# Repeating score fills ahead of the real ones, in place of zero-weight passes, in a gated mix of two attentions

## The chip, the cores and the metric

The kernel runs on one core of one Trainium2 chip. Its time is the device time of one execution in microseconds (us). The engines are named as in the profile: PE is TensorE (PEld its weight loads), ACT is ScalarE, DVE is VectorE, POOL is GpSimd and SP is SyncE. A profile adds one execution that was recorded instruction by instruction, and with it the share of its full clock that PE was granted from moment to moment.

## The reference

Two attentions over the same 2048 tokens of width 512, each with 32 heads of 16, are mixed by a gate for each token. Branch A is full attention without a mask, branch B looks at 8 earlier positions at a stride of 2.

```python
x = A_x                                                   # 1 x 2048 x 512, bf16
g = _sigmoid((x * gate_w).sum(-1, keepdims=True))
a = _A_ref(x, A_wqkv, A_wo)       # softmax(q k^T / 4) v over all 2048 keys, 32 heads of 16, then @ wo
b = _B_ref(x, B_wqkv, B_wo)       # the same with keys i, i-2, ... i-14 only, mask where < 0
return g * a + (1 - g) * b
```

Branch A is what costs most. Its scores are cut into units of 128 keys by 512 queries of one head: 16 blocks of keys, 4 chunks of queries and 32 heads make 2048 units. A unit is one matmul with a contraction of 32 rows ("score fill"), then 128 x 512 exponentials, then one matmul with the values (17 columns of weights, 16 of values and one of ones for the softmax's denominator).

## The kernel before

Branch A is worked in 32 periods: a chunk of 512 queries with a group of 4 heads, which is 64 units. The four heads of a group lie in the four row strips of 32 of PE's array (`tile_position=(32 * j, 0)`), so fills of different heads can stream side by side. Most units go to ACT in sets of three (ring A, three PSUM banks) and two (ring B, two banks) in turn: PE fills a ring, ACT takes the exponential of the whole ring in one instruction, and the ring is then free for the next fill. A part of the units ("riders") is filled beside a set into a bank of its own, and DVE takes the exponential there by a polynomial of four instructions. Projections, transposes and branch B's dot products lie in between.

The order of the instructions on each engine is not written by hand. When the program is built, a planner (`Plan`) plays the jobs through with an assumed duration for each step, and every engine's instructions are issued in the order in which the plan starts them. On the chip the engines run through these fixed orders and wait for each other by semaphores; the planned times themselves are not kept. A change of a planned duration can therefore move instructions of any job.

```python
class Plan:
    LAT = {"pe": 0.15, "act": 0.08, "dve": 0.08, "pool": 0.08, "sp": 0.08}
    streamed = deque()
    # ... (cut)
    def quiet(self, window):
        while self.streamed and self.streamed[0][0] < self.now - window:
            self.streamed.popleft()
        return sum(d - 0.11 for _, d in self.streamed)
    # ... (cut: run() picks the next step)
                if isinstance(more, float):
                    x[4] += more                      # a step may say that it takes longer
                if nm == "pe":
                    self.streamed.append((st, x[4]))  # what PE streamed, by the plan
```

The fills of the sets, the exponential, and where the ring comes free:

```python
    MM = 0.22; SW = 0.11; WARM = 0.47      # planned: one stream of 512 columns; a change of tiling

    def qk_mm(out_, p, t, j):
        c_, i = periods[p]
        mm(out_, kt_all[32 * j:32 * j + 32, i, t * 128:(t + 1) * 128], qt_tiles[p][32 * j:32 * j + 32, :],
           True, True, tile_position=(32 * j, 0))
    # ... (cut)
    def act_tail(k, parts, rname, rslot, ring, n):
        # ... (cut)
            A.activation(out=st["pT"][:, 0:n, :], in_=ring[:, 0:n, :], func=ACT.Exp,
                         scale=LN2 / 128.0, bias=-VOFF * LN2 / 128.0)
        yield ("act", k, 0.074 + 0.4267 * n, f)
        yield ("rel", rname, rslot)
    # ... (cut: then pv_job for the units of the set)
    def act_stream():
        while front[0] < NP:
            k = nset[0]
            nset[0] += 1
            rname = "rA" if k % 2 == 0 else "rB"
            slot = yield ("acq", rname, 0)
            want = 3 if k % 2 == 0 else 2
            # ... (cut: picks the units)
            dur = SW + MM

            def f():
                for s_, (p_, t, j) in enumerate(units):
                    qk_mm(ring[:, s_, :], p_, t, j)
                # ... (cut: riders)
            yield ("pe", 0, dur, f)
            yield ("spawn", act_tail(k, parts, rname, slot, ring, len(units)))
```

The matmuls with the values add up in one PSUM bank for each period (`acc`). The bank is opened by four passes with weights of zero (128 in the 32 periods). A fifth such pass may be added in a step, and adds zero to what is there:

```python
    def pv_job(p, items, res, prio, act=True):
        # ... (cut)
            extra = MM * (max(cnt) - 1)
            if P.quiet(3.0) + MM * max(cnt) < WARM * 3.0 and max(row_left[p]) > 0:
                j = max(range(4), key=lambda j_: row_left[p][j_])
                mm(acc[32 * j:32 * j + 32, :], z32[:], ones_t[:], False, False, tile_position=(0, 32 * j))
                extra += MM
                njunk[0] += 1
            return extra
```

## Time and profile before

| | |
|---|---|
| time, median of 3 runs | 944.16 us (941.46 to 947.36) |
| span of the profiled execution | 951.0 us, mean granted PE clock 0.842 |
| busy: ACT / PE / DVE / POOL | 851.9 / 800.1 / 762.0 / 582.7 us |
| sets on ACT | 369 of 3 and 2 units each in turn, 737 in all, 1842 units |
| units on DVE | 206 |
| zero-weight passes | 135, of which 128 open a period |

In the profile the groups of instructions are named by what they write and read: `ring<-qt,kt_all` is a score fill of a set, `w<-qt,kt_all` that of a rider, `pT<-ring` the exponential on ACT, `acc<-pT,vp_all` and `acc<-pd,vp_all` the matmuls with the values, `acc<-ones_t,z` a zero-weight pass. All carry the line of one helper, L252, so they are told apart by these names. A matmul's recorded duration [...]is longer than the time for which it keeps the array; matmuls overlap in the records. The row PEclk has the clock that PE was granted, in tenths of full speed.

### The profile page before, as it was taken

What the parts mean: (1) busy time and instruction counts of PE and PEld (TensorE: products, weight loads), DVE (VectorE), ACT (ScalarE), POOL (GpSimd) and SP (SyncE); (2) the same over time, 40 slices, a digit from 0 to 9 for tenths busy, and PEclk for the clock granted to TensorE, in tenths of its full rate; (3) what the DMA queues carried; (4) which work ended last, traced back from release to release, by engine and by line L of the source; (5) the groups of instructions that cost most, each with busy time, mean ns of one, the idle gap of its engine ahead of it and who ended that gap; (6) DMA issues with size and microseconds to landing.
All of it is one profiled execution on the core that took longest, in us unless ns stands there. A gap on an engine that the chain in (4) does not pass through costs nothing.

```text
span 951.0 us, 14436 instructions
## 1 busy us (share of the span) xinstructions
PE 800.1 (84%) x5415; PEld 233.3 (25%) x5415; DVE 762.0 (80%) x1326; ACT 851.9 (90%) x755; POOL 582.7 (61%) x543
## 2 busy tenths in 40 slices
PE   2889989988888888888978888888888988788986
PEld 0333433322222221222222222222122222222221
DVE  3568888868896899788886988788988789898784
ACT  0489899989999999899999989889989989999994
POOL 4005886347984999498949693919567662947000
PEclk9999999979879977778689967768788977876795
DMA  9004010121013303003030310203010230300000
GB/s 261 6 2 155 1 45 1 56 100 57 1 57 102 108 3 100 1 1 100 1 100 12 111 45 12 90 1 101 1 56 5 69 95 1 100 1 1 1 2 22
DMA packets 50007, 47.10 MB, mean 50 GB/s; under 512 B 9984, under 2 KB 47360, under 8 KB 49936
## 3 DMA queue, kind: packets, MB, share of 16 engines
q1 hardware_dynamic: 46240, 41.98, 14.6%
q10 hardware_dynamic: 3696, 4.20, 1.5%
q8 instruction: 42, 0.69, 0.3%
q14 instruction: 29, 0.24, 0.1%
HBM read 37.75 MB, written 6.32 MB: 46 GB/s over the span
## 4 chain that ended last, share of the span: by engine, by line
ACT 49%; PE 27%; issue 18%; DVE 4%; DMA 2%; SPq 0%; ACTq 0%; DVEq 0%
ACT pT L252 48%; PE w L252 11%; PE ring L252 9%; PE acc L252 7%; DMA xT<-in_A_x_dram 2%; DVE ta L252 2%; DVE pd L252 1%; ACT lg L252 0%; DVE kt_all L252 0%; DVE qt L252 0%; DVE vp_all L252 0%; DVE osb L252 0%; DMA out_dram<-osb 0%; SPq L252 0%; DVE accS L252 0%
## 5 line engine op out<-in xcount | busy, mean ns | idle before, releaser
L252 ACT ACTIVATE pT<-ring 128x1536 bf16<-128x1536 f32 x737 | 847.9, 1289 | 74.9 <-PE w L252 34.3
L252 PE MATMUL ring<-qt,kt_all 32*128 32x512 bf16 x1842 | 333.1, 444 | 115.2 <-ACT pT L252 107.4
L252 DVE SCALAR_TENSOR_TENSOR ta<-ta,w 128x512 f32<-128x512 f32 x412 | 278.2, 682 | 6.8
L252 PE MATMUL acc<-pT,vp_all 128*17 128x512 bf16 x1842 | 272.9, 450 | 0.4 <-ACT pT L252 0.2
L252 POOL TENSOR_TENSOR prod<-prod 128x512 f32<-128x512 f32 (+1 forms) x208 | 240.2, 1168 | 6.3
L252 POOL TENSOR_TENSOR prod<-vsh,lg 128x512 f32<-128x512 bf16 x128 | 136.6, 1099 | 174.0 <-issue 102.3
L252 POOL TENSOR_TENSOR prod<-ksh,qb 128x512 f32<-128x512 bf16 x128 | 143.6, 1154 | 104.0 <-DMA ksh<-kv_scr 94.1
L252 PEld LDWEIGHTS <-kt_all 32*128 32x128 bf16 x2048 | 92.3, 94 | 428.4 <-issue 421.8
L252 DVE TENSOR_SCALAR ta<-w 128x512 f32<-128x512 uint16 x206 | 141.4, 687 | 42.2 <-PE w L252 40.0
L252 DVE SCALAR_TENSOR_TENSOR pd<-ta,w 128x512 uint16<-128x512 f32 x206 | 139.8, 680 | 3.1
L252 PE MATMUL w<-qt,kt_all 32*128 32x512 bf16 x206 | 94.0, 458 | 0.0
L252 PE MATMUL acc<-pd,vp_all 128*17 128x512 bf16 x206 | 86.7, 475 | 0.0
L252 PEld LDWEIGHTS <-vp_all 128*17 128x17 bf16 x2048 | 46.2, 90 | 113.3 <-issue 111.8
L252 PE MATMUL w<-xT,wkp 128*128 128x512 bf16 x128 | 37.7, 423 | 19.0 <-DMA xT<-in_A_x_dram 17.2
L252 PE MATMUL w<-bw,xT 128*128 128x512 bf16 x192 | 51.4, 392 | 0.5 <-DVE otok L252 0.2
L252 PE MATMUL w<-xT,wqp 128*128 128x512 bf16 x128 | 50.2, 536 | 0.0
L252 DVE TENSOR_SCALAR absq<-w 128x512 int16<-128x512 int16 x32 | 22.1, 691 | 26.3 <-PE w L252 26.3
L252 DVE TENSOR_SCALAR kt_all<-w,kbias 128x512 bf16<-128x512 f32 x32 | 23.9, 748 | 23.5 <-PE w L252 23.4
L252 PEld LDWEIGHTS <-xT 128*128 128x128 bf16 x512 | 32.7, 103 | 37.0 <-issue 23.8
L252 DVE TENSOR_SCALAR qt<-w,qbias 128x512 bf16<-128x512 f32 x32 | 23.9, 748 | 14.9 <-PE w L252 14.9
L252 DVE COPY accS<-acc 128x512 f32<-128x512 f32 x32 | 22.0, 687 | 10.2 <-PE acc L252 10.2
L252 PE MATMUL w<-identf,accS 128*128 128x128 f32 x128 | 24.7, 324 | 3.7 <-DVE qt L252 2.7
(70 smaller groups left out, 412.5 us busy)
## 6 DMA issues: line engine op xcount, KB each, us to landing
ksh<-kv_scr SPq DMA_DIRECT2D x16, 1024.0 KB, 5.7
vsh<-kv_scr SPq DMA_DIRECT2D x16, 1024.0 KB, 6.8
kv_scr<-kvs SPq DMA_DIRECT2D x16, 256.0 KB, 2.0
out_dram<-osb SPq DMA_DIRECT2D x16, 128.0 KB, 1.8
bw<-in_B_wqkv_dram ACTq DMA_DIRECT2D x1, 1536.0 KB, 13.9
wraw<-in_A_wqkv_dram ACTq DMA_DIRECT2D x2, 512.0 KB, 5.5
wv<-in_A_wqkv_dram ACTq DMA_DIRECT2D x1, 512.0 KB, 9.2
bwo<-in_B_wo_dram ACTq DMA_DIRECT2D x1, 512.0 KB, 7.8
```

The source lines that it names most:

```text
L252: return chain_on(self._key, f(*a, **k))
```

## The change

The zero-weight pass inside a period goes. In its place the fill of a set may be issued twice: first over `n` columns, then over all 512. Both write the same banks with the same weights and the same queries, and the second overwrites the first, so that the computation is unchanged. The number of columns is the plan's shortage: how much less than 1.64 us PE would have streamed within the last 2.5 us, with `cur` for what it is about to stream before it next runs idle (one stream for a fill of three, three for a fill of two), in whole blocks of 64 columns and at most 512. The aim is to keep PE streaming in the stretches where it has little to do, as that of the zero-weight passes was.

```diff
+    REACH = 2.5
+    BUSY = 1.64
-    def quiet(self, window):
-
-        while self.streamed and self.streamed[0][0] < self.now - window:
+    def lack(self, cur):
+
+
+        while self.streamed and self.streamed[0][0] + self.streamed[0][1] < self.now - self.REACH:
             self.streamed.popleft()
-        return sum(d - 0.11 for _, d in self.streamed)
+        have = sum(min(d - 0.11, s + d - self.now + self.REACH) for s, d in self.streamed)
+        return self.BUSY - have - cur
 ...
+    def warm_cols(cur):
+
+        n = min(QW, -(-int(P.lack(cur) * 2400.0) // 64) * 64)
+        if n < 64:
+            return 0
+        njunk[0] += n / QW
+        return n
 ...
-    def qk_mm(out_, p, t, j):
+    def qk_mm(out_, p, t, j, n=QW):
         c_, i = periods[p]
-        mm(out_, kt_all[32 * j:32 * j + 32, i, t * 128:(t + 1) * 128], qt_tiles[p][32 * j:32 * j + 32, :],
+        mm(out_, kt_all[32 * j:32 * j + 32, i, t * 128:(t + 1) * 128], qt_tiles[p][32 * j:32 * j + 32, 0:n],
            True, True, tile_position=(32 * j, 0))
 ...
             extra = MM * (max(cnt) - 1)
-            if P.quiet(3.0) + MM * max(cnt) < WARM * 3.0 and max(row_left[p]) > 0:
-                j = max(range(4), key=lambda j_: row_left[p][j_])
-                mm(acc[32 * j:32 * j + 32, :], z32[:], ones_t[:], False, False, tile_position=(0, 32 * j))
-                extra += MM
-                njunk[0] += 1
             return extra
 ...
             def f():
+                n = warm_cols(MM if len(units) == 3 else 3 * MM)
+                if n:
+                    for s_, (p_, t, j) in enumerate(units):
+                        qk_mm(ring[:, s_, 0:n], p_, t, j, n)
                 for s_, (p_, t, j) in enumerate(units):
                     qk_mm(ring[:, s_, :], p_, t, j)
 ...
+                return n / 2400.0
             yield ("pe", 0, dur, f)
```

## The prediction

> **What bounds the kernel now.** I first read the page: busy shares, the row of PE's clock, and the chain that ended last.

> ```profile
> PE 800.1 (84%) x5415; PEld 233.3 (25%) x5415; DVE 762.0 (80%) x1326; ACT 851.9 (90%) x755; POOL 582.7 (61%) x543
> ...
> PEclk9999999979879977778689967768788977876795
> ...
> ACT 49%; PE 27%; issue 18%; DVE 4%; DMA 2%; SPq 0%; ACTq 0%; DVEq 0%
> ACT pT L252 48%; PE w L252 11%; PE ring L252 9%; PE acc L252 7%; DMA xT<-in_A_x_dram 2%; DVE ta L252 2%; DVE pd L252 1%; ACT lg L252 0%; DVE kt_all L252 0%; DVE qt L252 0%; DVE vp_all L252 0%; DVE osb L252 0%; DMA out_dram<-osb 0%; SPq L252
> ```

> ACT is the busiest engine and heads the chain; PE has 27% of it. PE's 84% says little, since records overlap and grow at a low clock. The clock is full for the first 200 us and then keeps falling: 23 stretches at half clock, 300.1 us in all. Next, the groups, and who waits for whom:

> ```profile
> L252 ACT ACTIVATE pT<-ring 128x1536 bf16<-128x1536 f32 x368 | 552.4, 1501 | 56.9 <-PE w L252 31.2 <-PE ring L252 17.1 <-PE acc L252 6.1
> L252 ACT ACTIVATE pT<-ring 128x1024 bf16<-128x1024 f32 x369 | 397.5, 1078 | 18.0 <-PE ring L252 12.8 <-PE w L252 3.1 <-PE acc L252 1.4
> ...
> L252 PE MATMUL ring<-qt,kt_all 32*128 32x512 bf16 x1842 | 333.1, 444 | 115.2 <-ACT pT L252 107.4 <-DVE qt L252 1.0
> ```

> ACT waits only for PE, and PE's fills wait only for ACT. When ACT sets the pace, starts of its records lie 0.903 us (two units) and 1.33 us (three) apart, 2.234 us for five units or 0.4467 us a unit. Who leads depends on the clock. Windows cut where the clock changes show it (columns: length; busy us of PE, PEld, DVE, ACT, POOL; granted clock; DMA):

> ```profile
> 275.50:343.70 68.20, 56.62 (x429) 18.73 (x422) 55.06 (x96) 67.77 (x62) 54.52 (x50) 1.00 0.25 74
> 367.60:391.50 23.90, 22.03 (x118) 4.50 (x117) 18.76 (x32) 21.46 (x20) 16.84 (x16) 0.50 0.29 89
> ...
> 678.20:698.70 20.50, 19.00 (x102) 3.67 (x101) 17.49 (x34) 18.67 (x17) 11.15 (x11) 0.50 0.00 1
> 893.30:924.00 30.70, 25.91 (x197) 8.27 (x196) 25.31 (x44) 30.70 (x29) 0.00 (x0) 1.00 0.00 1
> 924.00:951.00 27.00, 18.15 (x87) 3.82 (x86) 14.80 (x26) 14.93 (x14) 0.00 (x0) 0.50 0.06 20
> ```

> At full clock ACT is busy for 67.77 of 68.20 and 30.70 of 30.70 us; at half clock for 21.46 of 23.90 and 18.67 of 20.50. Over 100 to 924 us I divided ACT's units by the clock they fell under: 550.9 us at full clock for 1186.2 units, 0.4645 us a unit; 273.1 us at half clock for 505.1 units, 0.5406. ACT idles 9.1 us in the first and 33.9 us in the second. So this is an ACT-bound kernel that is PE-bound in a third of its time, because PE then runs at half speed.

> Last, why the clock falls: the timeline just before a fall (at 367.63 us).

> ```profile
> 365.40 0.40 PE L252 MATMUL ring<-qt,kt_all 32*128 32x512 bf16 x3 [0.42 <-ACT pT L252]
> ...
> 366.32 0.39 PE L252 MATMUL ring<-qt,kt_all 32*128 32x512 bf16 x2 [0.52 <-ACT pT L252]
> ...
> 366.64 0.60 PE L252 MATMUL acc<-pT,vp_all 128*17 128x512 bf16 x5
> ...
> 367.66 0.61 PE L252 MATMUL ring<-qt,kt_all 32*128 32x512 bf16 x3 [0.42 <-ACT pT L252]
> ```

> PE does the five units and nothing else, and waits 0.4 to 0.5 us before each fill. From the matmul records I laid 512 columns at full clock out as 0.213 us from each start, joined what overlaps, and cut the time into 3.41 us windows in phase with the falls. The 23 windows just before a fall are filled to 0.32 to 0.45; all that keep full clock except one lie at 0.45 or above, most at 0.5 to 0.6. In pulses of the full clock, windows split at about 0.42 to 0.43 whichever state they start in[...].

> [...]only 1.0 and 0.5 occur, for 3.41, 6.83, 10.24, 13.65 us and other multiples. [...]after 100 us the longest gap between matmul records is 1.0 us, and the clock falls 23 times[...]. [...]four `wqp` projections take 1.04 us with a last record of 0.39 at full clock and 1.89 with 0.61 at half, steps of 0.217 and 0.427[...]. [...]the three fills at 365.40 end together after 0.40 us, like one.

> **The change part by part.** I counted instructions in the built programs.

> *Removed:* 7 zero-weight passes beyond the 128 that open periods (135 to 128). 7 x 0.213 us lies in PE's waits: under 1 us, taken as nothing.

> *Added:* 451 score matmuls on 151 of the 738 fills: 115 fills of three over 512 columns, 34 of three and 2 of two over fewer, 64 to 448. Strips run side by side, so PE streams 115 x 0.213 = 24.5 us and, over 8512 columns in the other 36, 3.5 us more: 28 us.

> *Moved:* the plan now gives DVE 204 units and ACT 1844; two more units on ACT, 2 x 0.4467 = +0.9 us.

> *What the clock gives back.* First the 273.1 us: 505.1 units x (0.5406 - 0.4645) = 38.4 us. Then the last 27 us, all at half clock. About 14 us of them are still sets, some 2 us; the closing transposes (1.11 us against 0.66 for the same four at 919.06), output matmuls and value matmuls give about 1 us. In all 41.5 us if the clock never falls.

> *What remains cold.* I put the PE order of both programs at ACT's pace, 0.4467 us a unit, with 0.213 us a stream of 512 columns, and asked what share of 3.41 us windows stays under 0.43. It is 8.8% before and 2.1% after. Before, it is 3 to 4% in the first quarter, where the trace has no fall, and 9 to 13% later; after, it is 0 to 3% there. This is a count on fixed orders and ignores waits, so I take its ratio, about a quarter, and let a quarter of the 41.5 us stay: -31 us.

> *What the added fills cost.* They stand between the ring's release and its real fill. In the records of full-clock stretches a ring of three is refilled from 0.05 us after ACT leaves it, the fill takes 0.39 us, and ACT starts on it 0.27 us later (medians). Where ACT is visibly waiting the last step is 0.105 us. So the fill has 0.16 us to spare at the median, and 0 to 0.25 over the middle eight tenths. A repeat of 0.213 us thus delays ACT by about 0.05 us at the median, 0.08 us over all cases; they stand where PE has least to do and so most to spare. I take 0.055: 115 x 0.055 = 6.3 us, and nothing for the short ones.

> *Sum:* -31 + 6.3 + 0.9 = -24 us on the profiled span of 951.0. The timed runs are 7 us shorter than that execution, probably with fewer falls and so a little less to regain; I take -23 us off 944.2 and get **921 us**.

> **Rivals.** *(a) The repeats lie on the path.* If the spare time is gone where they are put, each costs its whole stream: 28 us in place of 6, and 943 us, no difference. For it: ACT does wait for `ring` and `w`, and a full repeat is longer than the median spare time. Against: before falls the fills themselves wait 0.4 to 0.5 us for ACT, so nothing queues ahead of them. *(b) The gate doesn't fully count them.* My split uses streamed time whatever rows and columns are in use, but windows that stay warm mostly hold projections on the whole array. Fitting separate weights, the split gets slightly cleaner if score fills count for less than the others. If half the cold time stays, it is -21 + 7, about 930 us. *(c) The clock never falls.* Then -41.5 + 7 or even less delay: about 907 us; the count of low windows, not zero, speaks against it. *(d) Another bound takes over.* DVE is busy for 55.06 of 68.20 us in the warm window, but its waits are for PE, and its share of units is fixed in the order; POOL ends before the last 75 us. I give this little.

> **Range and chances.** Between (c) and half of (a) lies 905 to 938 us, with the centre at 921. Two per cent is 925.3 us, a little above the centre: 0.62 for faster, 0.34 for the same, 0.04 for slower, which would need full repeats on the path and a clock that still falls.

> **What would show it.** The clock row should read 9 nearly throughout, with under 80 us at half clock; a quarter of 300 is the step to test. Units at full clock should pass at 0.465 us or up to 0.475; at 0.48 or more the repeats are on the path, and rival (a) holds. The fills' wait for ACT (107.4 us) should shrink as the repeats wait in their stead, and ACT's waits for `w`, `ring` and `acc` should fall by some 25 us. The last 27 us should begin at full clock. I am wrong if half-clock time stays above 150 us though the repeats run (rival b), or if it is gone and the time hardly moves (rival a).

## The result, and the profile after

The changed kernel takes 956.28 us (median of 4 runs, 949.41 to 957.18), the kernel before in the same measurement 944.5 us. The ratio is 1.0106 with a 95% interval of 1.0056 to 1.0155: about 1% slower, where 921 us were predicted.

The page of the changed kernel: busy shares, PE's clock, and the chain that ended last.

```profile
PE 770.0 (81%) x5859; PEld 238.9 (25%) x5859; DVE 761.1 (80%) x1318; ACT 850.1 (90%) x756; POOL 582.5 (61%) x543
...
PEclk8588999989997998996998999998998985997997
...
ACT 50%; PE 27%; issue 19%; DMA 2%; DVE 2%; ACTq 0%; SPq 0%; DVEq 0%
ACT pT L256 49%; PE ring L256 10%; PE w L256 10%; PE acc L256 6%; DMA xT<-in_A_x_dram 2%; DVE vp_all L256 0%; ACT lg L256 0%; DVE kt_all L256 0%; DVE osb L256 0%; DMA out_dram<-osb 0%; SPq L256 0%; DVE accS L256 0%; DVE ta L256 0%; DVE kmax
```

The clock did what the change was for, in part. After 55 us it is at half for 139.5 us in 20 stretches, against 302.0 us in 23 before (all such sums run to the end of the last clock record, 2 us past the last instruction). Yet PE still has 27% of the chain, and the groups of ACT show as much idle time as before (56.9 and 18.0 us there):

```profile
L256 ACT ACTIVATE pT<-ring 128x1536 bf16<-128x1536 f32 x369 | 549.5, 1489 | 53.4 <-PE ring L256 46.3 <-PE w L256 2.7 <-PE acc L256 1.5
L256 ACT ACTIVATE pT<-ring 128x1024 bf16<-128x1024 f32 x368 | 392.2, 1066 | 19.4 <-PE w L256 14.8 <-PE ring L256 3.9 <-PE acc L256 0.6
...
L256 PE MATMUL ring<-qt,kt_all 32*128 32x512 bf16 x2189 | 334.3, 411 | 130.5 <-ACT pT L256 125.6 <-DVE qt L256 1.0
```

Windows of the changed kernel (length; busy us of PE, PEld, DVE, ACT, POOL; granted clock; DMA):

```profile
15.00:35.00 20.00, 9.78 (x77) 5.31 (x78) 6.47 (x11) 0.00 (x0) 0.00 (x0) 0.57 0.61 142
506.00:628.90 122.90, 99.73 (x807) 31.23 (x808) 103.38 (x182) 121.74 (x110) 94.72 (x87) 1.00 0.17 52
785.90:806.40 20.50, 19.14 (x108) 3.92 (x107) 17.98 (x29) 18.39 (x17) 8.54 (x9) 0.50 0.00 1
936.10:947.50 11.40, 4.00 (x13) 1.45 (x12) 4.55 (x9) 0.00 (x0) 0.00 (x0) 0.50 0.14 48
```

Full clock for 123 us with ACT busy for all but 1.2 of them is what was hoped for. The first row needs a caution. The same window before reads full clock:

```profile
15.00:35.00 20.00, 9.93 (x81) 5.42 (x81) 7.16 (x12) 0.00 (x0) 0.00 (x0) 1.00 0.53 132
```

But the clock records of that execution begin only at 50.2 us, and what lies before the first record counts as full. Its timeline tells otherwise: four projections take 1.9 us, as in the changed kernel, where the record shows half clock (1.04 us at full).

```profile
20.74 1.89 PE L252 MATMUL w<-xT,wkp 128*128 128x512 bf16 x4 [6.07 <-DMA xT<-in_A_x_dram]
...
26.12 1.87 PE L252 MATMUL w<-xT,wkp 128*128 128x512 bf16 x4 [0.78 <-DVE vp_all L252]
```

So the start-up is at half clock in both, the mean clock of 0.842 given for the kernel before is too high, and from here on half-clock time is counted from 55 us.

Where did the time go? I noted when ACT started each unit. In the two profiled executions the changed kernel loses 12.8 us up to unit 161 (132.4 against 119.6 us) and 16.1 us up to unit 321, and gains it back later, in the stretches where the clock was low before. This pair flatters the change: the two executions took 949.4 and 952.7 us, while the medians are 956.3 and 944.5. The largest single loss is a stop of ACT near 100 us. Timeline of the kernel before there, PE and ACT:

```profile
93.62 0.39 PE L252 MATMUL ring<-qt,kt_all 32*128 32x512 bf16 x3
93.95 1.07 PE L252 MATMUL w<-wv,xT 128*128 128x128 bf16 x16
94.95 0.60 PE L252 MATMUL acc<-pT,vp_all 128*17 128x512 bf16 x5
95.48 1.04 PE L252 MATMUL w<-xT,wqp 128*128 128x512 bf16 x4
96.35 1.06 PE L252 MATMUL w<-wv,xT 128*128 128x128 bf16 x16
...
98.19 1.05 PE L252 MATMUL w<-wv,xT 128*128 128x128 bf16 x16 [0.52 <-DVE vp_all L252]
99.18 0.39 PE L252 MATMUL ring<-qt,kt_all 32*128 32x512 bf16 x2
...
99.69 1.02 ACT L252 ACTIVATE pT<-ring 128x1024 bf16<-128x1024 f32 x1 [3.86 <-PE ring L252]
```

And of the changed kernel, between the same two fills:

```profile
100.22 0.39 PE L256 MATMUL ring<-qt,kt_all 32*128 32x512 bf16 x3
100.55 1.04 PE L256 MATMUL w<-bw,xT 128*128 128x512 bf16 x4
101.51 0.60 PE L256 MATMUL acc<-pT,vp_all 128*17 128x512 bf16 x5
102.05 1.04 PE L256 MATMUL w<-xT,wkp 128*128 128x512 bf16 x4
...
103.33 1.04 PE L256 MATMUL w<-xT,wkp 128*128 128x512 bf16 x4
104.21 1.06 PE L256 MATMUL w<-wv,xT 128*128 128x128 bf16 x16
...
108.71 1.02 PE L256 MATMUL w<-xT,wqp 128*128 128x512 bf16 x4 [0.20 <-DVE vp_all L256]
109.57 1.06 PE L256 MATMUL w<-wv,xT 128*128 128x128 bf16 x16
...
111.41 1.03 PE L256 MATMUL w<-wv,xT 128*128 128x256 bf16 x8 [0.52 <-DVE vp_all L256]
112.38 0.39 PE L256 MATMUL ring<-qt,kt_all 32*128 32x512 bf16 x2
...
112.86 2.37 ACT L256 ACTIVATE pT<-ring 128x1024 bf16<-128x1024 f32 x2 [10.44 <-PE w L256]
```

No repeat stands in this stretch. Two sets of keys (`wkp`) and a projection with `bw`, which the order before has in earlier gaps, now stand here, and so do two groups of transposes that it has in later ones. ACT waits 10.4 us in place of 3.9. The order of the jobs moved.

### The profile page after: what moved, and what is told of

Read it like the earlier page. It is cut to its first block, busy times and chain, and to the rows that moved or that the text cites. A ratio compares the mean times of both kernels' runs of the same rounds, so it can differ in the third digit from the quotient of the medians.

```text
span 947.5 us, 15314 instructions
## 1 busy us (share of the span) xinstructions
PE 770.0 (81%) x5859; PEld 238.9 (25%) x5859; DVE 761.1 (80%) x1318; ACT 850.1 (90%) x756; POOL 582.5 (61%) x543
## 4 chain that ended last, share of the span: by engine, by line
ACT 50%; PE 27%; issue 19%; DMA 2%; DVE 2%; ACTq 0%; SPq 0%; DVEq 0%
ACT pT L256 49%; PE ring L256 10%; PE w L256 10%; PE acc L256 6%; DMA xT<-in_A_x_dram 2%; DVE vp_all L256 0%; ACT lg L256 0%; DVE kt_all L256 0%; DVE osb L256 0%; DMA out_dram<-osb 0%; SPq L256 0%; DVE accS L256 0%; DVE ta L256 0%; DVE kmax_all L256 0%; ACTq L256 0%
## 5 line engine op out<-in xcount | busy, mean ns | idle before, releaser
L256 ACT ACTIVATE pT<-ring 128x1536 bf16<-128x1536 f32 x738 | 845.9, 1277 | 72.8 <-PE ring L256 50.2
L256 PE MATMUL ring<-qt,kt_all 32*128 32x512 bf16 (+1 forms) x2295 | 338.1, 405 | 142.2 <-ACT pT L256 136.7
L256 PE MATMUL acc<-pT,vp_all 128*17 128x512 bf16 x1844 | 249.6, 414 | 0.6 <-ACT pT L256 0.4
L256 PEld LDWEIGHTS <-kt_all 32*128 32x128 bf16 x2499 | 101.7, 92 | 435.3 <-issue 424.8
L256 PE MATMUL w<-qt,kt_all 32*128 32x512 bf16 x204 | 84.2, 413 | 0.0
L256 PE MATMUL acc<-pd,vp_all 128*17 128x512 bf16 x204 | 79.3, 419 | 0.0
L256 PE MATMUL w<-xT,wqp 128*128 128x512 bf16 x128 | 36.4, 411 | 0.2 <-DVE vp_all L256 0.2
L256 DVE COPY accS<-acc 128x512 f32<-128x512 f32 x32 | 21.9, 685 | 13.0 <-PE acc L256 12.8
L256 DVE CAST kvs<-w 128x512 bf16<-128x512 f32 x32 | 21.9, 686 | 9.9 <-PE w L256 8.6
```

Source lines behind the costliest of these rows:

```text
L256: return chain_on(self._key, f(*a, **k))
```

## The experiments

Ratios are to the kernel before, run beside each group on the same chip (medians 943.1, 944.8, 946.7, 943.7 and 947.5 us for the five groups). "Half" is the time at half clock after 55 us in the profiled execution. In all variants the added matmul is overwritten by the real fill, so that the computation is the same. The medians are of all executions, while the ratios leave out those more than 1.5% above the kernel's fastest; the profiled executions of the kernel before (953 us), e10 (952 us) and e13 (945 us) are of that kind, and e14's (942 us) is its longest.

| kernel | us | ratio (95%) | half, us |
|---|---|---|---|
| changed kernel | 956.3 | 1.0106 (1.0056 to 1.0155) | 139.5 |
| e1 its order, no repeats | 970.0 | 1.0303 (1.0240 to 1.0366) | 307 |
| e2 repeats, plan not charged | 934.7 | 0.9923 (0.9895 to 0.9951) | 126 |
| e3 repeats, charged from period 9 | 951.5 | 1.0070 (1.0037 to 1.0103) | 174 |
| e4 neither | 942.3 | 1.0006 (0.9985 to 1.0028) | 274 |
| e5 as e2, whole-array matmul | 930.2 | 0.9844 (0.9813 to 0.9874) | 91 |
| e6 as e2, target 2.0 us | 921.5 | 0.9770 (0.9691 to 0.9850) | 47 |
| e7 as e2, zero pass 128 x 32 | 915.8 | 0.9726 (0.9632 to 0.9819) | 20 |
| e8 as e5, target 2.0 us | 921.6 | 0.9769 (0.9696 to 0.9841) | 24 |
| e9 as e7, charged | 939.2 | 0.9921 (0.9879 to 0.9963) | 57 |
| e10 as e7, target 1.4 us | 948.9 | 0.9991 (0.9951 to 1.0031) | 221 |
| e11 as e2, one fill repeated | 970.8 | 1.0288 (1.0202 to 1.0375) | 290 |
| e12 as e7, non-zero data | 931.1 | 0.9844 (0.9793 to 0.9895) | 99 |
| e13 as e9, charged in periods 1 to 8 | 937.9 | 0.9946 (0.9902 to 0.9990) | 109 |
| e14 as e9, charged from period 9 | 936.5 | 0.9938 (0.9909 to 0.9966) | 132 |
| e15 as e9, keys sooner | 944.3 | 1.0014 (0.9986 to 1.0041) | 99 |
| e16 as e7, keys sooner | 942.1 | 0.9990 (0.9959 to 1.0022) | 94 |
| e17 as e7, again | 921.8 | 0.9686 (0.9602 to 0.9770) | 20 |
| e18 as e12, again | 928.3 | 0.9804 (0.9739 to 0.9869) | 20 |

### Order or repeats?

Theory M: the repeats lengthen PE's steps in the plan, the plan then puts other jobs elsewhere, and that order costs time. Rival P, my rival (a): the repeats themselves hold up ACT.

**e4**, the base: the zero-weight pass inside a period is gone and nothing is put in its place (`if P.quiet(3.0) ...` to `njunk[0] += 1` left out).

> Neither repeats nor the 7 added zero-weight passes: the base of the two before. Both theories: 941 to 949 us, within 0.5% of the kernel before, since 7 passes are 1.5 us of PE.

942.3 us, no difference from before (the interval holds 1). The removal is free, and e4 is the base for what follows. Its order is not quite that of the kernel before: PE's instructions are the same up to the 1656th matmul and differ in places after it.

**e1**, the order alone:

```diff
                 n = warm_cols(MM if len(units) == 3 else 3 * MM)
-                if n:
-                    for s_, (p_, t, j) in enumerate(units):
-                        qk_mm(ring[:, s_, 0:n], p_, t, j, n)
+                # the plan is charged for the repeat; it is not issued
 ...
                 return n / 2400.0
```

> The order of the changed kernel on every engine, with none of its 451 repeated score matmuls issued. Theory M (what the change costs is the order: the plan charges PE 28 us more and puts off the first periods' projections): the early stops of ACT stay (some 10 us near 100 us, 4 us near 67 us) and the clock falls as often as before, so 950 to 962 us. Rival P (the repeats delay ACT on the chip, the order is harmless): 940 to 948 us, as before.

970.0 us, slower than M's range. The order on every engine is exactly that of the changed kernel, and it costs 970.0 - 942.3 = 27.7 us without a single repeat. ACT's stop near 100 us is there in full:

```profile
110.84 2.37 ACT L256 ACTIVATE pT<-ring 128x1024 bf16<-128x1024 f32 x2 [11.07 <-PE w L256]
```

In this order the repeats help: the changed kernel's ratio is 2.0% under e1's. P falls as the cause of the loss.

**e2**, the repeats alone. The rule and its bookkeeping stay, but the step's planned length doesn't grow. The order on every engine is e4's but for the repeats, which are 470 matmuls on 157 fills in the built program (the expectation below counts 462).

```diff
-                return n / 2400.0
+                P.extra = n / 2400.0
+                return 0.0
 ...
-                    self.streamed.append((st, x[4]))
+                    self.streamed.append((st, x[4] + self.extra))
+                    self.extra = 0.0
```

> The repeats are issued by the same rule (462 matmuls on 157 fills), but the plan is not charged for them, so that apart from them the order is that of a kernel with neither repeats nor zero-weight passes. Theory M: the gain of the clock without the early loss, 922 to 936 us, half-clock time under 180 us. Rival P: 948 to 960 us, as the changed kernel.

934.7 us, 0.8% faster than before: M's direction, at the slow end of its range. The gain over e4 is 7.6 us although half-clock time went from 274 to 126 us. What a repeat costs can be read in its timeline. The first two lines are at full clock, the others at half; x6 is a fill with its repeat, x3 one without.

```profile
643.39 0.61 PE L258 MATMUL ring<-qt,kt_all 32*128 32x512 bf16 x6 [0.41 <-ACT pT L258]
...
647.91 0.40 PE L258 MATMUL ring<-qt,kt_all 32*128 32x512 bf16 x3 [0.42 <-ACT pT L258]
...
704.57 1.04 PE L258 MATMUL ring<-qt,kt_all 32*128 32x512 bf16 x6 [0.23 <-ACT pT L258]
...
705.71 2.37 ACT L258 ACTIVATE pT<-ring 128x1536 bf16<-128x1536 f32 x2 [0.28 <-PE ring L258]
...
708.43 0.61 PE L258 MATMUL ring<-qt,kt_all 32*128 32x512 bf16 x3
```

At full clock a whole repeat adds 0.21 us, and the fill had been waiting 0.41 us for ACT anyway. At half clock it makes the fill 1.04 us long, and ACT shows a wait for it. I took ACT's delay ahead of each set of three (spacing of the starts less 0.903 us for the set of two before it): with a whole repeat it is 0.026 us on average at full clock (88 sets, 2.2 us in all), and 0.386 us at half clock (30 sets, 11.6 us). At half clock the sets of e4, without repeats, lose 0.208 us on average, and those that carry a repeat in e2 only 0.10 us (76 sets). So the repeats make the cold stretches that remain dearer: units pass there at 0.569 us against 0.521 in e4. Between 100 and 924 us, 141.8 us less at half clock should give 15 us by e4's own rates (0.4647 and 0.5206 us a unit); the dearer cold units take back 201 x 0.048 = 10 us, the slightly slower warm ones (0.4659) 2 us. That leaves a gain of 3 to 4 us in this stretch.

**e3**, repeats charged to the plan, but none before the ninth period (`if units[0][0] >= 8 else 0`).

> The change, repeats charged to the plan, but only from the ninth of the 32 periods on, when the projections of keys and values are done. Theory M: the early order is as without repeats, so 925 to 940 us. Rival P: the repeats that remain (about 390 matmuls) cost as before, 945 to 958 us.

951.5 us: M's expectation missed. The number lies in P's range, but e1 and e2 have ruled P out as the cause. The early order is unspoilt and the stop near 94 us is at its 4.2 us, yet the ratio is 1.5% above e2's. The order costs later too, so M's "first periods" was too narrow.

### What holds the clock up?

By the gate I mean whatever sets PE's clock; the runs show only the clock granted. e2 left 126 us at half clock where a quarter of 274 was due. In the changed kernel 15 of the 21 windows ahead of a fall stream 0.43 or more, past my split; before, 3 of 23 do. Theory G, my rival (b): a score fill does less for the clock than other matmuls. Rival T: only streamed time matters. Each variant stands in the same places as e2, with the order of e2.

**e11**, one of the two or three fills repeated; **e5**, one matmul of 128 x 128 weights; **e7**, one pass of 128 x 32 zero weights over ones; **e12**, the same shape with key weights and `x`:

```diff
-                    for s_, (p_, t, j) in enumerate(units):
-                        qk_mm(ring[:, s_, 0:n], p_, t, j, n)
+e11                 p_, t, j = units[0]
+e11                 qk_mm(ring[:, 0, 0:n], p_, t, j, n)
+e5                  c_, i_ = periods[units[0][0]]
+e5                  mm(ring[:, 0, 0:n], wkp[:, 0, i_].rearrange("p j d -> p (j d)"),
+e5                     xT[:, 0, c_ * QW:c_ * QW + n], True, True)
+e7                  mm(ring[0:32, 0, 0:n], z32[:], ones_t[:, 0:n], True, True, tile_position=(0, 0))
+e12                 c_, i_ = periods[units[0][0]]
+e12                 mm(ring[0:32, 0, 0:n], wkp[:, 0, i_, 0, :], xT[:, 0, c_ * QW:c_ * QW + n], True, True,
+e12                    tile_position=(0, 0))
```

> As the uncharged repeats, but only the first of a set's two or three fills is repeated; PE streams for the same time, on 32 rows in place of 64 or 96. If a repeat counts by the rows in use: half-clock time up from 126 us towards 200 us and 937 to 945 us. If it counts by streamed time: within 0.5% of the 934.7 us of the uncharged repeats.

> As the uncharged repeats, in the same 157 places and over the same columns, but each repeat of two or three score fills is one matmul of a 128 x 128 weight block (its result is overwritten). PE streams for the same time. Theory G (the clock's gate counts a score fill of 32 rows a strip for less than a matmul on the whole array): half-clock time well under the 150 us of the uncharged repeats, under 90 us, and 922 to 931 us. Rival T (only streamed time counts): the same within 0.5%, 931 to 939 us, and the same half-clock time.

> As the uncharged repeats, in the same places, but each repeat is one pass of 128 x 32 zero weights into a strip of the ring's first bank (overwritten by the fill). If the gate counts streamed time alone: as the uncharged repeats, 931 to 939 us. If it counts what the array does, zeros or 32 of 128 columns count for little: half-clock time 200 us or more and 938 to 948 us.

> As the zero-weight passes in the ring, but the 128 x 32 block of weights is part of the key weights and the moving operand is x, so that the shape is the same and the data aren't zero and one. If shape decides (128 rows on 32 columns, and the change of tiling around it): 913 to 920 us and half-clock time under 50 us, as with zeros. If zeros and ones were what made the passes count more[...]: 924 to 936 us.

The windows from 55 to 910 us, one line each (columns as above: the figure after POOL's is the clock). First e4, without anything added,

```profile
55.00:910.00 855.00, 727.99 (x5002) 214.46 (x5065) 714.53 (x1245) 815.59 (x724) 571.85 (x528) 0.86 0.15 47
```

The same window of e11, 32 rows,

```profile
55.00:910.00 855.00, 746.25 (x5060) 214.28 (x5058) 698.44 (x1213) 795.77 (x704) 572.23 (x528) 0.85 0.15 47
```

the same of e2, 96 rows in three strips (64 in the one repeat of a set of two),

```profile
55.00:910.00 855.00, 713.37 (x5499) 222.78 (x5563) 722.59 (x1258) 821.76 (x732) 571.89 (x528) 0.94 0.15 47
```

and of the 128-row passes of e7 in their second measurement (e17):

```profile
55.00:910.00 855.00, 700.58 (x5259) 213.38 (x5322) 730.36 (x1274) 832.80 (x740) 572.08 (x528) 0.99 0.15 47
```

The fillers run over the same columns in all but e4, which has none. With 32 rows they lift the clock not at all (290 us at half against 274), and at half clock each delays ACT (0.37 us on average over 71 sets of three, against 0.10 in the same sets of e4): 970.8 us, slower than nothing added. With 96 rows half-clock time is halved (126 us); with 128 rows it is 91 us (e5), 20 (e7) and 99 (e12). ACT does 724 instructions in this window in e4, 704 in e11 and 740 in e17. T is refuted, and G holds in this form: the more rows in use, the less half-clock time was left. e5 (weights of 128 columns) and e12 (32) have the same ratio, 0.9844, so no effect of the weights' columns shows. From 32 to 96 rows nothing else about the matmuls changes but their number (1 or 3), and one pass of 128 rows left less than three fills did (20 to 99 us against 126). From 96 to 128 rows the tiling of the array changes too: e5, e7 and e12 switch it ahead of the fill, e2 doesn't. In e7 a whole pass starts 0.31 us ahead of its fill (887.00 and 887.31 us), where a whole repeat in e2 adds 0.21. What the switch does to the clock was not separated.

The windows ahead of the falls, laid out as in the prediction, agree. In e11, 18 of 24 stream 0.43 or more, up to 0.50; in e4 none of 22 does, in e12 2 of 11. So the split at 0.42 to 0.43 belongs to one mix of matmuls. No single share marks the recovery either: in e4's profile the clock comes back after windows that stream 0.70 to 0.87 (0.427 us for 512 columns, the step at half clock), and stays low after others of 0.62 to 0.83.

My expectation for e7, half-clock time of 200 us or more with zeros or few columns, was the wrong way round: it is 20 us. To see whether zeros do more for the clock, e7 and e12 ran once more side by side, five rounds each:

> The uncharged zero-weight passes in the ring once more, beside their twin. If the 915.8 us belong to the kernel: 913 to 922 us and a ratio to the kernel before of 0.968 to 0.978. If they belonged to the chip: 926 to 936 us, like the twin's 931.1.

> The twin with key weights and x in the pass, same shape, places and chip. If zeros and ones count more in the gate: 927 to 935 us and at least 1% over the zero-weight passes. If the chip made the difference: within 0.5% of them.

921.8 and 928.3 us, and the two profiled executions are alike: spans of 913.8 and 913.6 us, four falls and 19.6 us at half clock in each. One execution differs from the next with its mean granted clock (for e17 914 to 916 us at 0.974 to 0.977, and 928 to 930 us at 0.957 to 0.962; for e18 915 us at 0.974, and 927 to 932 us at 0.933 to 0.968), and the intervals of the two overlap. That zeros do more is not shown. That the passes beat both kernels is: 0.9726 and 0.9686 in two measurements. e5, e7 and e12 differ from one another by less than such executions do.

### How much streaming?

**e6**, **e8** and **e10** change `BUSY` alone: 2.0 with the repeats of e2, 2.0 with the whole-array matmul of e5, 1.4 with the passes of e7.

> As the uncharged repeats, with the target raised from 1.64 to 2.0 us in 2.5 us: 211 fills of three and 104 of two carry a repeat, 242 of these over all columns. Theory G: more streaming of the weak kind still lifts the clock, half-clock time 40 to 110 us; a repeat costs ACT 0.01 to 0.03 us at full clock but 0.39 us at half, so with fewer cold stretches 926 to 936 us. Rival P (repeats on the path): slower than the uncharged repeats, over 940 us.

> The whole-array matmul in place of each repeat, at the target of 2.0 us (315 places). Theory G: the clock hardly falls after the first 50 us, half-clock time under 55 us, and what is left is the order's own stops: 918 to 928 us. Rival T: as the target of 2.0 us with score fills, within 0.5%.

> Zero-weight passes in the ring, uncharged, at a target of 1.4 us in place of 1.64. If the passes count double or more in the gate, fewer are enough: 913 to 919 us with half-clock time under 60 us. If the count in planned streaming was what mattered: 922 to 932 us, as the uncharged repeats at 1.64 or a little better.

The target of 2.0 puts a filler on 339 fills in the built programs (239 of three, 100 of two), more than the 315 that the expectations count. With enough repeats the weak filler does as well as the strong one: 921.5 us (e6) and 921.6 us (e8). A whole repeat ahead of a set of three still costs only 0.037 us on average at full clock (174 sets in e6). This is the clearest evidence against P, and against "no filler of this kind can pay". The passes on 128 rows cost more there, 0.08 us (115 sets in e7). e10 missed: at 1.4 us the passes leave 221 us at half clock and 948.9 us. Fewer passes are not enough.

### Which part of the order?

**e9** charges the plan for e7's passes, so that it has the changed kernel's order. **e13** and **e14** charge it in the first 8 periods only, or only after them (`return n / 2400.0 if units[0][0] < 8 else 0.0`, and `>= 8`).

> The changed kernel and its order (repeats charged to the plan), but each repeat is one zero-weight pass of 128 x 32 in the ring. Theory M+G (the change lost in two ways, by its order and by a filler that the gate counts for little): the clock stays up (half-clock time after 55 us under 50 us), the early stops of ACT stay, so about 15 to 25 us over the 915.8 us of the same passes uncharged: 930 to 941 us. Rival (the order only costs where the clock is low): under 924 us.

> Zero-weight passes in the ring, charged to the plan in the first 8 of the 32 periods alone. The early order is that of the changed kernel: 8.1 us of PE work between fills 46 and 47, against 4.05 uncharged. Theory M: the early part is the larger half of the 23.5 us that the charge costs, 926 to 935 us. Rival (the loss is spread over all periods): 916 to 924 us.

> The same passes, charged only from the ninth period on; the early order is the uncharged one. Theory M: 918 to 926 us. Rival (spread): 930 to 938 us.

e9 takes 939.2 us: with the clock at half for only 57 us in its profile, the order still costs about 2% (0.9921 against 0.9726 and 0.9686). To see where, I added up over each profiled execution, from 55 to 924 us, how much later than its pace ACT started each set (0.903 us after a set of two, 1.331 us after a set of three), and split the sum by the clock:

| kernel | late at full clock, us | late at half clock, us |
|---|---|---|
| e4 neither | 24.7 | 40.2 |
| e1 changed order, no repeats | 37.0 | 55.8 |
| e7 passes, uncharged | 37.3 | 2.0 |
| e9 passes, charged | 45.4 | 9.2 |
| e14 charged from period 9 | 32.9 | 29.4 |
| e15 keys sooner, charged | 43.2 | 19.6 |
| e16 keys sooner, uncharged | 47.0 | 16.5 |

The window of e9, to be read beside that of e17 above:

```profile
55.00:910.00 855.00, 706.37 (x5259) 210.96 (x5258) 722.18 (x1251) 826.18 (x734) 572.05 (x528) 0.98 0.15 47
```

e9 loses 8.1 us more than e7 at full clock, 6.8 of them in the stop near 97 us (11.1 us against 4.3), and 7.2 us more at half clock, with 9 falls against 4. e1 loses 12.3 us more than e4 at full clock, 6.9 of them in the same stop, and 15.6 us more at half. So the rival "only where the clock is low" falls, but about half of the order's cost does lie there.

e13 and e14 take 937.9 and 936.5 us. Each half of the charge costs as much as the whole, so the loss is neither early nor late, and it doesn't add up. In e14 the early order is untouched and nothing more is lost at full clock, but the clock falls 12 times in place of 4, and 29.4 us are lost at half clock against 2.0.

**e15** and **e16** give the third head group's keys a higher priority, charged and uncharged:

```diff
-            P.spawn(k_job(i, sc, ev_start[i - 1], 10 + 0.1 * sc))
+            P.spawn(k_job(i, sc, ev_start[i - 1], (5 if i == 2 else 10) + 0.1 * sc))
```

> The passes charged everywhere, with the third head group's key projections at a higher priority, so that the gap between fills 46 and 47 holds 1.7 us of PE work in place of 8.1 (and that between 57 and 58 3.2 us). Theory M: the 11 us stop near 97 us goes, and the time falls by 7 to 12 us from 939 us, to 927 to 933 us. Rival: another stop takes its place, 936 to 942 us.

> The uncharged passes with the same higher priority: here the plan then heaps 7.25 us of PE work between fills 52 and 53 and leaves 4.05 us less between 46 and 47. Theory M: a stop of ACT of about 8 us near 108 us, net 3 to 7 us slower than the 915.8 us of the uncharged passes, 918 to 924 us. Rival: order does not matter while the clock is up, within 0.5%.

e15 did to the stop what it should: near 97 us ACT loses 3.5 us and near 111 us 3.9 us, where e9 lost 11.1. But the time is 944.3 us, and the ratio 0.9% above e9's. Its rival holds: other stops and falls take their place (half-clock time 99 us against 57). e16 has the expected stop (9.3 us at 99.9 us), but its ratio is 2.6% above e7's, some 25 us rather than 3 to 7; its clock falls 11 times against 4, with the same rule for passes.

So M stands in what it says of the order (e1, e9), and falls in where it put the loss. All five orders other than e4's that I ran with 128-row passes lose 2 to 3% against it. The stop near 100 us is one visible piece, some 7 us; most of the rest lies at half clock. Which step of an order makes the clock fall wasn't found. Nor do the runs tell whether e4's order is a rare good one or the five share a fault; the order of the kernel before, different from e4's in places, takes the same time.

## Why the prediction was wrong

- **What bounds the kernel.** Right in kind: ACT sets the pace at full clock (0.471 us a unit in the changed kernel, predicted 0.465 to 0.475), PE at half (0.5707 us a unit). "The clock is full for the first 200 us" was wrong for the first 50, which have no records.
- **Moved: +0.9 us.** The step that failed. I counted what the plan gave to ACT and DVE, and took the order of all else as unchanged in cost. Alone it costs 27.7 us (e1 against e4): in the profiles 12 us at full clock, most of it the stop near 100 us, and 16 us at half. Under a filler that nearly holds the clock it still costs about 2% (e9 against e7 and e17). I had compared the streaming of both orders, but not what stands between two fills.
- **What the clock gives back: 41.5 us.** Too large. The 0.5406 us a unit at half clock came from one profiled execution; e4, a kernel of the same time, shows 0.5206 in its own. Most of all, the units left at half clock get dearer by the repeats (0.5707 in the changed kernel), as worked out for e2.
- **What remains cold: a quarter.** Measured 139.5 of 302 us, nearly half. The count of windows under 0.43 took each streamed column as equal. The same columns left 290 us as fills of one strip (e11), 126 in three strips (e2) and 91 on 128 rows (e5); the fit in rival (b) had pointed that way.
- **What the added fills cost: 0.055 us each, 6.3 us.** At full clock it is even less: 0.025 us over 81 whole repeats, 2.0 us. At half clock, which I left out, 33 repeats cost 0.383 us each, 12.6 us. The 0.213 us that I took for a stream of 512 columns is half the step of 0.427 us at half clock; four projections in a row show 0.217 at full clock.
- **The signs.** With 139.5 us at half clock and 0.471 us a unit, neither limit at which I would have called myself wrong (150 us, 0.48 us) was passed: none of the signs watched the order. The last 27 us did begin at full clock, which held until 936.1 us. The fills' wait for ACT should have shrunk from 107.4 us; it grew to 136.7. ACT's waits for `w`, `ring` and `acc` should have fallen by 25 us from 71.6; they are 69.9:

```profile
PE ring L256 <- ACT pT L256: 136.7, 349, 1.2
...
ACT pT L256 <- PE ring L256: 50.2, 52, 23.3
...
ACT pT L256 <- PE w L256: 17.6, 6, 10.4
...
ACT pT L256 <- PE acc L256: 2.1, 10, 0.3
```

  The longest of these are the wait for the first fill (23.3 us) and the stop near 100 us (10.4).
- **Rivals.** (a) fell as the cause of the loss; e6 with twice the repeats is faster still. (b) was right: fills of 32 rows a strip left more half-clock time than matmuls on 128 rows (126 us in e2 at a ratio of 0.9923, 91 in e5 at 0.9844). The one that decided, an order that costs more than the clock gives, was not among them. By ratios: +3.0% for the order (e1), -2.0% for the repeats in it, together +1.1%.

## What to carry to other kernels

Where a planner sets the order, a filler charged to it is two changes in one: measure the new order with the filler left out and the filler with the order kept. Where a filler is to hold PE's clock, try its rows in use besides its columns: here the same columns on 32, 96 and 128 rows left 290, 126 and 20 to 99 us at half clock, though more columns on 96 rows left 47 (e6). A filler that fits the spare time at full clock may not fit at half: a whole repeat delayed ACT by 0.026 and by 0.386 us (e2), and by my estimate there the dearer units took back 12 of the 15 us that the clock gave.
